# A scan with expert routing: PSUM banks dealt out anew, another order of its loop, other places for loads and weight splits

## The chip, the cores and the metric

The kernel runs on one core of a Trainium2 chip. The metric is the device time of one execution in microseconds (us). All times below are in us unless marked ns. TensorE does the matrix products, VectorE, ScalarE and GpSimd the elementwise work, and SyncE (SP) issues most of the transfers. PSUM, into which TensorE writes, has eight banks.

## The reference

Three stages run one after the other, for 4 batches of 768 positions. The first is a chunked scan with 8 heads (head width 32, state width 16):

```python
log_a = np.log(np.clip(a, 1e-06, 1.0))
for c in range(nc):                                   # chunks of the sequence
    cum = np.cumsum(la, axis=-1)
    L = np.exp(cum[:, :, :, None] - cum[:, :, None, :]) * causal
    y_intra = einsum((Cc @ Bc^T) * L, xc)
    y_inter = einsum(Cc, state) * np.exp(cum)
    state = decay_full * state + sum_j(Bc_j xc_j * decay_from_j)
```

The second is a mixture of 8 experts on the scan's output (256 columns). Each token's expert is the argmax of its 8 logits, or, where a gate lies at 0.5 or above, the expert of the token before it, so the choice is itself a scan over the sequence. The result is `p[e] * (relu(x @ w1[e]) @ w2[e])`. The third adds the real part of a Fourier transform over the sequence and the columns, normalizes, and adds a two-layer product.

## The kernel before

`phase_a` (line 170) holds the scan and the routing; then come the eight experts (line 802), and the third stage (line 1055). Each engine works through its instructions in the order in which the program lists them (`manual_schedule`), and waits only where data or a buffer asks for it.

In `phase_a` the sequence is cut into 6 chunks `c` of 128 positions. One iteration `i` of the loop at line 623 handles a pair: one chunk and two of the four batches (`bp`), so there are 12. Per pair: `prep` makes two masked copies `ch` of `ce` (the C rows times the decay rows), `scores` (line 338) multiplies them with the B rows into four PSUM banks `g0` to `g3`, `mask` (line 352) puts the causal mask on them on VectorE, `carry` (line 361) adds the state's part to `yb`, `intra` (line 373) the masked product with `xt`, `keep` (line 384) copies `yb` out on ScalarE, and `rows` (line 423) turns that copy into rows of tokens with their logits in `tl`, two groups of two products each, which ScalarE copies to `x1n`. `state_mm`, `state_up`, `state_add` and `state_scale` renew the state through `dps`. `xt` (line 332), `ce` (line 277) and `state_add` run on GpSimd.

PSUM: `yb` has two banks. Its first 256 columns per bank take `carry` and `intra`. Its free columns hold `rp` (the routing's transposes), `dps`, `lp` and `rk_ps` (the ranks). Where TensorE writes one bank and another engine reads it, the program makes them wait for each other, whatever the columns are. `tl` has two buffers of one bank.

The decay rows: `decays` works them out from `a` into `e_r`, which is stored to HBM (`e_d`) and loaded again spread over 128 partitions by `load_eb` (line 267), eight transfers of 32 KB for each chunk, in pieces of 512 bytes; chunk 0 is spread by a product instead (`spread0`). The buffers for it in the pool `ald` are two. `load(c)` (line 187) loads the inputs of a chunk into one of three sets of buffers.

Routing: `routing` (line 439) is a generator for one chunk (for the last chunk, half of one). Its steps on VectorE are handed out by `gap`, some between the four masks of an iteration; its steps on TensorE by `place`: the transposes of `kd` (line 469), those of `er` (line 490), and the ranks: a product with `tri` (line 506), one with the counts so far (line 507), and three products (line 513) over the tiles of the chunk. Each product in 32-bit floats stands as two instructions in the trace. At the end each chunk has four scatters (line 556, two with each `leave`) of its token rows to `xs_buf`, sorted by expert; the experts load from there (`xn`, line 732), and that load waits for all 24 scatters.

`load_w` (line 130) loads an expert's two weights into the two buffers `raw`; its generator then splits each into a high part (ScalarE, line 149) and a low part (VectorE and GpSimd, line 151), in four steps. For expert 0 the steps stand at the ends of the iterations 6 to 9. `zfill` (line 300) fills with zeros the rows of `xs_buf` that may stay unused.

## Time and profile before

| | us |
|---|---|
| median of 3 runs (lowest to highest) | 514.0 (511.27 to 516.89) |
| the profiled execution's own time | 515.08 |
| its span, first to last instruction | 513.3 |
| TensorE busy in the span | 466.0 (91%) |
| VectorE busy | 260.0 (51%) |
| ScalarE busy | 191.0 (37%) |
| GpSimd busy | 210.5 (41%) |
| mean granted TensorE clock, as a share of 2.4 GHz | 0.939 |

A busy share is an average over stages with different limits. A row of the timeline names the start, the duration, the engine, the line, the operation, the tile written and the tiles read, and in brackets how long the engine had been idle before and who released it. Durations of merged rows span all their instructions. The products' ends are modelled.

### The profile page before, as it was taken

How to read it: one execution, taken by the hardware profiler on the slowest of the kernel's cores; microseconds unless marked ns; L12 is line 12 of the kernel's file. 1: busy time of each engine (PE TensorE's matmuls, PEld its weight loads, DVE VectorE, ACT ScalarE, POOL GpSimd, SP SyncE). 2: the span in 40 equal slices, each digit the busy share in tenths (PEclk: the TensorE clock that was granted, in tenths of full speed). 3: DMA queues.
4: the chain of work that ended last, by engine and by line, in shares of the span. 5: the costliest groups of instructions: out<-in, count | busy, mean ns of one | idle time of the engine just before them, and what ended most of it. 6: DMA issues, size and time to landing. Idle time of an engine off the chain costs nothing. (4 is left out here: it accounts for less than half of the span.)

```text
span 513.3 us, 9012 instructions
## 1 busy us (share of the span) xinstructions
PE 466.0 (91%) x3481; PEld 396.5 (77%) x3481; DVE 260.0 (51%) x652; ACT 191.0 (37%) x393; POOL 210.5 (41%) x233
## 2 busy tenths in 40 slices
PE   8786787776699999999999999779999999999996
PEld 4564556464389989898989989466898989898986
DVE  3553495533164635455364633098655657574341
ACT  2253253211155454545455443124433243443130
POOL 2233377517138474655738463275430333220000
PEclk9797998565899999999999999989999999999999
DMA  7595823302314553544354410360022201000001
GB/s 242 180 244 162 289 104 125 121 15 91 112 41 130 162 195 131 177 144 144 137 165 134 162 61 18 97 215 23 1 70 104 92 2 43 1 26 17 32 10 43
DMA packets 36899, 54.73 MB, mean 107 GB/s; under 512 B 4013, under 2 KB 27725, under 8 KB 36848
## 3 DMA queue, kind: packets, MB, share of 16 engines
q1 hardware_dynamic: 33296, 46.40, 28.7%
q0 software_dynamic: 3072, 7.46, 4.3%
q8 instruction: 29, 0.48, 0.4%
q10 hardware_dynamic: 480, 0.22, 0.2%
q14 instruction: 22, 0.18, 0.1%
HBM read 42.24 MB, written 12.87 MB: 107 GB/s over the span
## 5 line engine op out<-in xcount | busy, mean ns | idle before, releaser
L703 DVE SCALAR_TENSOR_TENSOR hl<-mm,hh 128x512 fp32r<-128x512 f32 x112 | 77.1, 690 | 77.0 <-ACT hh L702 76.9
L702 ACT ACTIVATE hh<-mm 128x512 fp32r<-128x512 f32 x112 | 66.5, 596 | 90.7 <-PE mm L701 90.7
L710 PE MATMUL mm<-w2h,hh 128*128 128x256 f32 x256 | 72.1, 282 | 0.0
L710 PE MATMUL mm<-w2l,hh 128*128 128x256 f32 x256 | 71.5, 279 | 0.0
L710 PE MATMUL mm<-w2h,hl 128*128 128x256 f32 x256 | 71.5, 279 | 0.0
L750 POOL DMA_INDIRECT y_tok<-y,ids x32 | 34.4, 1076 | 53.1 <-ACT y L749 33.0
L710 PE MATMUL mm<-c2h,hh 128*128 128x256 f32 x192 | 54.4, 284 | 0.0
L710 PE MATMUL mm<-c2h,hl 128*128 128x256 f32 x192 | 53.8, 280 | 0.0
L710 PE MATMUL mm<-c2l,hh 128*128 128x256 f32 x192 | 53.8, 280 | 0.0
L701 PE MATMUL mm<-xh,w1h 128*128 128x512 f32 x128 | 50.9, 398 | 0.0
L701 PE MATMUL mm<-xh,w1l 128*128 128x512 f32 x128 | 50.8, 397 | 0.0
L710 PEld LDWEIGHTS mm<-w2h,hl 128*128 128x128 f32 x256 | 48.5, 189 | 0.0
L710 PEld LDWEIGHTS mm<-w2l,hh 128*128 128x128 f32 x256 | 48.2, 188 | 0.0
L710 PEld LDWEIGHTS mm<-w2h,hh 128*128 128x128 f32 x256 | 48.2, 188 | 0.0
L151 POOL TENSOR_TENSOR w1l<-r,w1h 128x640 fp32r<-128x640 f32 x16 | 30.5, 1905 | 37.8 <-ACT w1h L149 37.8
L701 PE MATMUL mm<-xl,w1h 128*128 128x512 f32 x128 | 40.1, 395 | 0.0
L701 PE MATMUL mm<-xh,c1h 128*128 128x512 f32 x96 | 39.4, 411 | 0.6 <-ACT xh L724 0.6
L701 PE MATMUL mm<-xh,c1l 128*128 128x512 f32 x96 | 38.0, 396 | 0.0
L710 PEld LDWEIGHTS mm<-c2l,hh 128*128 128x128 f32 x192 | 36.2, 188 | 0.1
L710 PEld LDWEIGHTS mm<-c2h,hh 128*128 128x128 f32 x192 | 36.1, 188 | 0.1
L710 PEld LDWEIGHTS mm<-c2h,hl 128*128 128x128 f32 x192 | 36.2, 188 | 0.0
L355 DVE TENSOR_TENSOR mt<-g,ca 128x512 f32<-128x512 f32 x48 | 31.1, 681 | 8.7 <-PE g L346 8.6
(306 smaller groups left out, 904.0 us busy)
## 6 DMA issues: line engine op xcount, KB each, us to landing
r<-in_w_dram SPq DMA_DIRECT2D x16, 1024.0 KB
xn<-xs_buf SPq DMA_DIRECT2D x8, 530.0 KB
rawc<-in_wc_dram SPq DMA_DIRECT2D x8, 512.0 KB
out_dram<-o SPq DMA_DIRECT2D x24, 128.0 KB
z<-y_tok SPq DMA_DIRECT2D x3, 768.0 KB
xs_buf<-scr SPq DMA_DIRECT2D x8, 265.0 KB
c1h<-in_x_dram SPq DMA_DIRECT2D x4, 512.0 KB
xk<-y_tok SPq DMA_DIRECT2D x4, 512.0 KB
```

What stands on the lines that cost most here:

```text
L151: eng.tensor_tensor(out=l_[:, x:y], in0=r_[:, x:y], in1=h[:, x:y], op=ALU.subtract)
L355: V.tensor_tensor(out=m[:, :, 2 * q:2 * q + 2, :], in0=gp[q], in1=cc("cmask").unsqueeze(1).unsqueeze(1).to_broadcast([128, 2, 2, 128]), op ...
L701: PE.matmul(out=ps, lhsT=w[:, d, f * 128:(f + 1) * 128], rhs=x[:, d, :], start=(k == 0), stop=(k == 5))
L702: A.activation(out=hh[:, f, :], in_=ps, func=ACTF.Relu)
L703: V.scalar_tensor_tensor(out=hl[:, f, :], in0=ps, scalar=0.0, in1=hh[:, f, :], op0=ALU.max, op1=ALU.subtract)
L710: PE.matmul(out=ps, lhsT=h[:, f, t * 128:(t + 1) * 128], rhs=w[:, f, :], start=(k == 0), stop=(k == 23))
L750: w = G.indirect_dma_start(out=y_tok, out_offset=bass.IndirectOffsetOnAxis(ap=ids[:, t:t + 1], axis=0), in_=y, in_offset=None, bounds_chec ...
```

## The change

- `rp`, `dps`, `lp`, `rk_ps` and the counts move from `yb` to a bank of their own, `mb`; `tl` has one buffer instead of two.
- `decays`, `columns` and the spreading of chunks 0 and 1 (`spread01`) come in halves, interleaved with the first scores; chunk 1's decay rows no longer go through HBM.
- `e_d` is laid out so that `load_eb` reads pieces of 2 KB; all its 32 transfers stand ahead of the loop, with four buffers. The zero fills move from before the loop into its first four iterations.
- In the loop `mask`, `state_up`, `rows` (now one group per call) and `carry` change places; `place` stands twice between the two groups of `rows`; `gap` gives steps first to chunks that had no `place` in this iteration. The additional `place` calls of the last two iterations go.
- Ranks: one scan over expert and tile (`ac`) replaces three products and the steps `at` and `an`.
- Weights: expert 0's two loads at the iterations 5 and 7, its first two splits at 8 and 9, the other two behind the last scatters; expert 1's loads at 10 and 11. `fa`, `fb`, `rix` at 9 instead of 7.

The diff, cut to its core:

```diff
-            ld = st.enter_context(tc.tile_pool(name="ald", bufs=2))
+            ld = st.enter_context(tc.tile_pool(name="ald", bufs=4))
...
-            rp, dps = yb[:, 0, 256:512], yb[:, 1, 256:384].rearrange("p (u d) -> p u d", u=2)
+            mb = pg.tile([128, 512], FP32, name="mb")
+            rp, dps = mb[:, 0:256], mb[:, 256:384].rearrange("p (u d) -> p u d", u=2)
...
-            warm(4)
+            warm(2)
...
+            def spread01(c, part):
+                ps0 = yb[:, c, :].rearrange("p (b i) -> p b i", b=NB)
+                r = 32 * c
+                if part == 0:
+                    ces[c] = wk.tile([128, NB, 128], FP32, tag="ce", name="ce")
+                for b in range(2 * part, 2 * part + 2):
+                    PE.matmul(
+                        out=ps0[:, b, :], lhsT=bsel[r:r + 32, b, :], rhs=e_r[r:r + 32, 0, 0:128], start=True, stop=True
                     )
+                h = slice(2 * part, 2 * part + 2)
+                V.tensor_tensor(out=ces[c][:, h], in0=ps0[:, h], in1=lds[c]["ct"][:, h], op=ALU.mult)
...
                     SP.dma_start(
-                        out=ebs[c][16 * h:16 * h + 16],
-                        in_=e_d[c * NB:(c + 1) * NB, h, :].unsqueeze(0).to_broadcast([16, NB, 128]),
+                        out=ebs[c][16 * h:16 * h + 16].rearrange("n b i -> n (b i)"),
+                        in_=e_d[c, h].rearrange("b i -> (b i)").unsqueeze(0).to_broadcast([16, NB * 128]),
                     )
...
-                    tl = pg.tile([128, RW], FP32, tag="t", name="tl", bufs=2)
+                tl = pg.tile([128, RW], FP32, tag="t", name="tl")
...
-                oh = sm.tile([128, nb, NE], FP32, tag="oh", name="oh")
+                ot = sm.tile([128, NE, nb + 1], FP32, tag=f"ot{nb}", name="ot")
+                oh = ot[:, :, 1:].rearrange("p e b -> p b e")
                 V.tensor_tensor(out=oh, in0=tb, in1=f_.to_broadcast([128, nb, NE]), op=ALU.is_equal)
+                yield "v", lambda: route["a"] == (c, b0)
+                V.tensor_copy(out=ot[:, :, 0], in_=route["acc"])
                 yield
-                ac = route["acc"]
+                ac = sm.tile([128, NE, nb + 1], FP32, tag=f"ac{nb}", name="ac")
+                V.tensor_tensor_scan(
+                    out=ac.rearrange("p e b -> p (e b)"), data0=again[nb].rearrange("p e b -> p (e b)"),
+                    data1=ot.rearrange("p e b -> p (e b)"), initial=0.0, op0=ALU.mult, op1=ALU.add,
+                )
...
+                PE.matmul(out=rk_ps, lhsT=cc("tri"), rhs=oh, start=True, stop=False)
                 PE.matmul(
-                    out=rk_ps, lhsT=cc("ones"), rhs=ac.unsqueeze(1).to_broadcast([128, nb, NE]),
-                    start=False, stop=False, skip_group_check=True,
-                )
-                for b in range(nb - 1):
-                    n = nb - 1 - b
-                    PE.matmul(
-                        out=rk_ps[:, b + 1:nb, :], lhsT=cc("ones"), rhs=oh[:, b:b + 1, :].to_broadcast([128, n, NE]),
-                        start=False, stop=(n == 1), skip_group_check=True,
-                    )
+                    out=rk_ps, lhsT=cc("ones"), rhs=ac[:, :, 0:nb].rearrange("p e b -> p b e"), start=False, stop=True
+                )
...
-                        if r[1] is None:
+                    for r in sorted(rq, key=lambda r: r[3] == now[0]):
+                        if r[1][0] == "v" and r[1][1]():
...
+            decays(0, 0)
+            spread01(0, 0)
+            spread01(0, 1)
             prep(0)
+            decays(0, 1)
+            columns(0)
             prep_x(0)
+            scores(0)
             prep(1)
             prep_x(1)
-            scores(0)
-            load(1)
-            load_eb(1)
+            decays(1, 0)
+            for q in range(6):
+                SP.dma_start(
+                    out=e_d[q].rearrange("h b i -> b h i"), in_=e_r[32 * (q % 3):32 * (q % 3) + 32, q // 3, 0:128]
+                )
             load(2)
-            load_eb(2)
-            zfill(0)
-            zfill(4)
-            mask(0)
+            for q in range(2, 6):
+                load_eb(q)
+            state_mm(0)
+            for q in range(4):
+                mask(0, q)
+            state_up(0)
+            spread01(1, 0)
+            spread01(1, 1)
+            decays(1, 1)
             kappa0()
             kappa()
+            columns(1)
...
                     load(c + 2)
-                    load_eb(c + 2)
-                if i in (4, 10):
-                    ws = load_w(i // 10)
-                if i == 7:
+                if i < 4:
+                    zfill(2 * i)
+                    zfill(2 * i + 1)
+                if i in (5, 7):
+                    ws = load_w(0, i // 7)
+                if i in (10, 11):
+                    ws1 = load_w(1, i - 10)
+                if i == 9:
...
                 intra(i)
                 keep(i)
-                if more and pairs[i + 1][0] + 1 < NC:
+                if more:
+                    mask(i + 1, 0)
+                    gap(1)
+                    mask(i + 1, 1)
+                    mask(i + 1, 2)
+                if upd:
                     state_mm(i + 1)
+                    state_up(i + 1)
+                if more:
+                    mask(i + 1, 3)
+                rows(i, 0)
                 place()
-                rows(i)
                 place()
+                rows(i, 1)
+                if more:
+                    carry(i + 1)
                 state_add(i)
                 state_scale(i)
...
                 leave()
-                gap(6)
-                if i + 2 >= NP:
-                    place()
-                    gap(4)
-                    place()
-                    if more:
-                        carry(i + 1)
+                gap(7)
...
+                gap(3)
+                if bp == 1 and c + 2 < NC:
+                    spread(c + 2)
+                if i in (8, 9):
+                    next(ws)
...
             while scq:
                 leave(0)
+            for _ in ws:
+                pass
```

## Rows read from the trace of the kernel before

**Rows 1.** Windows by stage: busy of each engine, clock, DMA share, GB/s

```profile
16.30:38.64 22.34, 19.20 (x345) 14.64 (x339) 11.82 (x28) 10.79 (x29) 7.51 (x8) 0.85 0.90 228
38.64:107.69 69.05, 52.31 (x640) 38.54 (x636) 37.79 (x107) 23.63 (x63) 34.05 (x43) 0.79 0.47 149
107.69:130.42 22.73, 15.91 (x86) 10.71 (x83) 6.33 (x49) 2.85 (x12) 13.73 (x21) 0.59 0.19 67
```

**Rows 2.** Windows of three single iterations, the same columns (PE, PEld, DVE, ACT, POOL)

```profile
28.46:33.52 5.06, 4.25 (x93) 3.26 (x89) 3.15 (x10) 2.65 (x8) 1.46 (x2) 1.00 1.12 181
38.64:49.66 11.02, 6.72 (x93) 5.04 (x89) 3.71 (x10) 3.27 (x11) 3.06 (x5) 0.77 0.60 171
92.06:107.69 15.63, 12.20 (x89) 8.62 (x85) 9.06 (x34) 2.40 (x7) 6.67 (x9) 0.50 0.33 103
```

**Rows 3.** Timeline of an undisturbed iteration, TensorE's products and ScalarE's two copies

```profile
28.46 1.15 PE L346 MATMUL g<-ch,c2h 32*128 32x256 f32 x16
...
29.54 1.08 PE L379 MATMUL yb<-mt,xt 128*32 128x128 f32 x32
...
30.69 0.60 ACT L386 ACTIVATE x1t<-yb 128x512 f32<-128x512 f32 x1 [1.05 <-PE yb L379]
...
31.43 0.43 PE L394 MATMUL yb<-xt,c2l 128*32 128x64 f32 x16 [0.81 <-ACT x1t L386]
...
31.79 1.20 PE L433 MATMUL tl<-ca,x1t 128*128 128x137 f32 x8
...
32.56 0.86 ACT L437 ACTIVATE scr<-tl 128x265 f32<-128x265 f32 x2 [1.28 <-PE tl L433]
...
32.92 0.67 PE L368 MATMUL yb<-ce,st 32*64 32x128 f32 x16
```

**Rows 4.** Timeline of two stalls: the decay rows, and carry behind the routing

```profile
42.88 1.26 POOL L277 TENSOR_TENSOR ce<-eb,c1l 128x512 f32<-128x512 f32 x1 [7.32 <-DMA eb<-e_d]
...
44.17 0.91 ACT L324 ACTIVATE ch<-ce,ca 128x256 f32<-128x256 f32 x2 [5.16 <-POOL ce L277]
...
56.84 0.67 PE L368 MATMUL yb<-ce,st 32*64 32x128 f32 x16 [0.51 <-ACT kr L479]
```

**Rows 5.** Waits of VectorE, 16 to 111: total, times, longest

```profile
DVE ro L521 <- PE yb L368: 12.2, 2, 7.4
```

**Rows 6.** Timeline of SyncE's queue: start, time over which issued, count

```profile
9.94 5.47 SPq L270 DMA_DIRECT2D eb<-e_d  x8
...
23.83 5.06 SPq L303 DMA_DIRECT2D xs_buf<-scr  x8
...
33.14 7.96 SPq L270 DMA_DIRECT2D eb<-e_d  x8
...
96.48 0.38 SPq L136 DMA_DIRECT2D r<-in_w_dram  x1
132.13 0.92 SPq L732 DMA_DIRECT2D xn<-xs_buf  x2
```

**Rows 7.** All transfers into `eb`: duration of one issue, ns, least, median, most

```profile
L270 SPq DMA_DIRECT2D eb<-e_d x38: 302/414/1038, 9.9 to 59.0; - x38
```

**Rows 8.** Timeline of the prologue, VectorE's second reciprocal

```profile
5.97 0.95 DVE L247 RECIPROCAL e_r<-f_r 96x128 f32<-96x128 f32 x1 [0.44 <-ACT e_r L232]
```

**Rows 9.** Groups by line and form, 16.3 to 107.69: busy, mean ns, idle before

```profile
L355 DVE TENSOR_TENSOR mt<-g,ca 128x512 f32<-128x512 f32 x44 | 28.6, 681 | 6.4 <-PE g L346 6.3
L513 PE MATMUL yb<-oh,cb 128*128 128x24 f32 x8 | 2.0, 328 | 0.0
```

**Rows 10.** Groups of GpSimd by line, 16.3 to 131, the same columns

```profile
L556 POOL DMA_INDIRECT xs_buf<-scr,si x24 | 24.1, 1006 | 7.8 <-issue 5.2 <-POOL scr L554 2.6
L151 POOL TENSOR_TENSOR w2l<-r,w2h 128x640 fp32r<-128x640 f32 x2 | 3.1, 1544 | 4.9 <-ACT w2h L149 4.8
```

**Rows 11.** Timeline of the tail: the last scatter, and the first work on `xn`

```profile
129.42 0.97 POOL L556 DMA_INDIRECT xs_buf<-scr,si  x1 [0.30 <-issue]
...
136.30 0.16 DVE L739 SCALAR_TENSOR_TENSOR ids<-xn,out_of 128x4 int32<-128x4 int32 x1 [10.62 <-DMA xn<-xs_buf]
```

More of the change, by code (lines that the diff above doesn't have):

```diff
@@ L228, in phase_a, with decays @@
             f_sb = big.tile([128, 24, NH], FP32, name="f_sb")
-            e_d = dram.tile([24, NH, 128], FP32, name="e_d")
+            e_d = dram.tile([NC, NH, NB, 128], FP32, name="e_d")
             lt = big.tile([96, 2, 64], FP32, name="lt")
             V.memset(zz, 0.0)
-            A.activation(out=e_r[:, 0, 0:1], in_=zz[:, 0:1], func=ACTF.Exp)
+            tw = big.tile([96, 1], FP32, name="tw")
+            A.activation(out=tw, in_=zz[:, 0:1], func=ACTF.Exp)
             V.memset(f_r[:, :, 63:64], 1.0)
-            def decays():
-                V.tensor_scalar(out=ar, in0=ar, scalar1=1e-6, scalar2=1.0, op0=ALU.max, op1=ALU.min)
-                for q in range(2):
+            def decays(q, part):
+                if part == 0:
+                    V.tensor_scalar(out=ar[:, q], in0=ar[:, q], scalar1=1e-6, scalar2=1.0, op0=ALU.max, op1=ALU.min)
                     V.tensor_tensor_scan(
@@ L243, in decays @@
                     )
-                V.tensor_copy(out=f_r[:, :, 0:63], in_=lt[:, :, 1:64])
-                V.tensor_copy(out=e_r[:, :, 128:129], in_=lt[:, :, 0:1])
-                V.reciprocal(out=f_r[:, :, 64:128], in_=e_r[:, :, 64:128])
-                V.reciprocal(out=e_r[:, :, 0:64], in_=f_r[:, :, 0:64])
-            def columns():
-                for q in range(2):
-                    ps0 = pg.tile([128, 512], FP32, tag="t", name="ps0", bufs=2)
-                    PE.transpose(ps0[:, 0:96], f_r[:, q, :], ident[0:96, 0:96])
-                    A.activation(
-                        out=f_sb[:, 12 * q:12 * q + 12, :].rearrange("p u h -> p (u h)"), in_=ps0[:, 0:96], func=ACTF.Copy
-                    )
@@ L257, in phase_a @@
-            ces, ebs = {}, {}
-            def spread0():
-                ps0 = pg.tile([128, NB, 128], FP32, tag="t", name="eb", bufs=2)
-                for b in range(NB):
-                    PE.matmul(out=ps0[:, b, :], lhsT=bsel[:, b, :], rhs=e_r[0:32, 0, 0:128], start=True, stop=True)
-                ces[0] = wk.tile([128, NB, 128], FP32, tag="ce", name="ce")
-                V.tensor_tensor(out=ces[0], in0=ps0, in1=lds[0]["ct"], op=ALU.mult)
+                    V.tensor_copy(out=f_r[:, q, 0:63], in_=lt[:, q, 1:64])
@@ new lines, in decays, with columns @@
+                    V.reciprocal(out=e_r[:, q, 0:64], in_=f_r[:, q, 0:64])
+                else:
+                    V.reciprocal(out=f_r[:, q, 64:128], in_=e_r[:, q, 64:128])
+                    V.tensor_copy(out=e_r[:, q, 128:129], in_=lt[:, q, 0:1])
+            def columns(q):
+                ps0 = pg.tile([128, 512], FP32, tag="t", name="ps0")
+                PE.transpose(ps0[:, 0:96], f_r[:, q, :], ident[0:96, 0:96])
+                A.activation(
+                    out=f_sb[:, 12 * q:12 * q + 12, :].rearrange("p u h -> p (u h)"), in_=ps0[:, 0:96], func=ACTF.Copy
+                )
@@ L530, in routing @@
                 )
-                yield
-                at = sm.tile([128, NE], FP32, tag="at", name="at")
-                V.tensor_reduce(out=at, in_=oh.rearrange("p b e -> p e b"), axis=AX.X, op=ALU.add)
-                yield
-                an = sm.tile([128, NE], FP32, tag="ac", name="ac")
-                V.tensor_tensor(out=an, in0=ac, in1=at, op=ALU.add)
-                route["acc"] = an
-                route["a"] = (c, 2) if nb < NB and not b0 else (c + 1, 0)
                 yield
@@ L569, in step @@
                 try:
[L570 removed]
+                    r[1] = next(r[0]) or ("v", lambda: True)
                 except StopIteration:
@@ L585, in place @@
                 for r in sorted(rq, key=lambda q: q[2]):
-                    if r[1] is not None and r[1]():
+                    if r[1][0] == "p" and r[1][1]():
+                        r[3] = now[0]
                         step(r)
@@ L634, in phase_a @@
                     SP.dma_start(out=rix, in_=io["rix"])
+                upd = more and pairs[i + 1][0] + 1 < NC
                 if more:
@@ L659, in phase_a @@
                 leave()
-                gap(6)
-                if i + 2 >= NP:
-                    place()
-                    gap(4)
-                    place()
-                    if more:
-                        carry(i + 1)
-                if bp == 1 and c + 2 < NC:
-                    spread(c + 2)
+                gap(7)
                 if c + 1 == NC:
```

122 lines of the change are left out of this document (58 added, 64 removed).

## The prediction

> **What bounds the kernel now.** I read the windows by stage first. The first expert's matmuls start at 137.86; what comes before is the scan with the routing, and only there does the diff touch anything. In [rows 1] look at TensorE's busy time beside the length of each stretch, and at the granted clock behind it. The two expert stages after 137.86 are left alone, so every gain or loss is a shift of that start. The chain of waits as answered reaches back only to the late expert stages, so the scan is read from windows and timelines.
>
> The loop has twelve iterations (pairs of batches). Eleven of them, from the scores of the second pair at 16.30 to the last `intra` at 107.69, take 22.34 for the first four and 69.05 for the next seven, 9.86 each [rows 1]. In those seven no engine is full: over seven iterations TensorE 52.31 (7.5 each, at a mean clock of 0.79, so about 5.9 at the full 2.4 GHz), VectorE 37.79 (5.4), GpSimd 34.05 (4.9), ScalarE 23.63 (3.4). So waits bound it, and a clock that falls in them. [rows 2] shows both ends: an undisturbed iteration takes 5.06 at clock 1.00, one with the inputs late 11.02 at 0.77, the last but one 15.63 at 0.50 (1.2 GHz).
>
> The undisturbed one [rows 3] is a chain on TensorE: scores, intra, a hole of 0.74 (31.43 less 30.69) while ScalarE copies `yb` out, then state products, the two `tl` rows, carry. State products wait for that copy although they read nothing of it: `dps` lies in the same bank.
>
> Two stalls recur. The decay rows arrive late: `ce` waited for `eb`, ScalarE's `ch` for `ce`, and the copy of `yb` stands behind `ch` on ScalarE [rows 4]. And the routing shares `yb` with the state: carry waits for ScalarE's reading of `kr` [rows 4], VectorE's `ro` for carry, up to 7.4 at once and 12.2 in two waits [rows 5], and all masks stand behind `ro` on VectorE; scores and intra wait for masks. The SP queue shows the first stall's root: eight zero fills issued from 23.83, then the inputs of chunk 3, and its `eb` loads only from 33.14 to 41.10 [rows 6].
>
> **The change, part by part.** *Prologue.* `e_r` of the first half no longer waits for both full reciprocals (0.95 for the second, behind a wait of 0.44 for ScalarE's table load, [rows 8]); half a reciprocal remains before `spread01`. That frees the 0.44, the 0.95 of the first (of the same size), half of the second and some of the scans, 2.3. Against it, chunk 1's `ce` in two halves and the last half reciprocal now stand before the first scores of the loop, about 1.1 with their hand-offs. I take 1.2 earlier; ends 2.3 earlier and 1 later.
>
> *First four iterations.* No stall to remove in most; they pay the single `tl` bank. `tl` had two buffers, now one: the second row group waits for ScalarE's copy of the first. From [rows 3]: half of 1.20 is 0.60, so the first would end at 32.39; ScalarE starts at 32.56 (0.17 later), needs 0.43, and some 0.14 pass until TensorE resumes (x1t ends at 31.29, L394 starts at 31.43): 0.74. Queued behind it are the second `tl`, carry and the next scores. Against it the state products (0.36 until `tl` starts) move into the hole, since `dps` is in `mb` now. Net 0.4 per iteration: 1.6 lost.
>
> *The seven.* 5.06 + 0.4 = 5.46. Routing on TensorE fills the new hole first, since both `place` calls stand between the two row groups. Of the rank products the L513 group goes, six instructions per chunk, of which the two of one form cost 2 x 328 ns [rows 9], 2.0 per chunk as recorded and mostly at the low clock; about 0.8 at the full one. What is left, some 1.4 per chunk or 0.7 per iteration, lies in a hole of 0.74, but unevenly; I add 0.25: 5.7. VectorE does four masks of 681 ns [rows 9] first and routing after them; its load of 5.4 falls a little, because two of the four splits of expert 0's weights move behind the loop; the new copy and scan take the place of `at` and `ac`. Where the scan of `er` waits for `kr` it lags by some 0.4: 6.1. GpSimd: 34.05 less two splits (3.1), plus 3.7 of issue time about its twelve scatters, is 34.7, 5.0 each [rows 1, 10]. But a chunk's four scatters (1.0 and 0.3 of issue each, [rows 10]) fall into one iteration, and the last `ce` stands behind them on GpSimd, `ch` and the copy of `yb` behind `ce` on ScalarE: I take 2 once, between nothing and 5.2. Sum 7 x 6.1 + 2 = 44.7 against 69.05, a gain of 24.3. The bounds: 5.06 each (35.4), and 8 each (56) if half of today's waiting returns.
>
> *Decay rows.* Chunk 1's come by matmul. The other four chunks' `eb` loads go out at once, before the zero fills, since `ald` has four buffers. Eight of them took 5.47 to issue with inputs ahead and 7.96 behind the zero fills [rows 6]; one alone takes 414 ns in the median [rows 7]. After the first eight (done about 16, since the inputs of chunk 2 stand before them) 24 more cost 10 to 16, four zero fills 2.5, so chunk 3's inputs go out between 29 and 35; they are needed at some 38. I count the stall as gone; if the slow issue holds, up to 4 comes back. The Trainium skill (DMA: Bandwidth & Descriptors, Measured) speaks against this part: transfers under 64 KB are dominated by their descriptors, and an `eb` transfer stays at 32 KB whatever its pieces. By that rule the rows would be no sooner, and the sum would be 504 instead of 500. No row shows 2 KB pieces of this transfer.
>
> *Tail.* Twelve scatters remain when the loop ends, before and after: the last ends at 130.39 [rows 11], 22.7 behind 107.69. The extra `place` calls of the last two iterations are gone, so chunks 4 and 5 have two to three routing steps more to do behind the loop. A copy out of PSUM with its two hand-offs is 0.74 [rows 3], with VectorE's part about 1 per step: 3 later; ends 0 and 5.
>
> *Weights.* Half of expert 0's splits now run on GpSimd behind the last scatter: 2 x 1.54 [rows 10] plus hand-offs, 3.4. The second weight half of expert 1 reuses the buffer they read, so its transfer waits for them, and on the SP queue the load of `xn`, which the first expert needs, stands behind that transfer. Before, it had gone out at 96.48, and `xn` at 132.13, 1.74 after the last scatter [rows 6, 11]. Now `xn` goes out some 4.1 after it: 2.4 lost. Then 1 MB is ahead of it in the queue. Both `xn` loads, 1.06 MB, were in by 136.30, at most 4.2 after their issue [rows 6, 11]; the megabyte costs between 2 and 4.2; I take 3.6. Together 6 (ends 2.4 and 6.6).
>
> **Sum**: -1.2 + 1.6 - 24.3 + 3 + 6 = -14.9. Against the profiled execution's 515.08 (its span 513.3 and 1.8 around it) that is 500; it lies 1.1 above the median of 514.0, so 499 to 500 there. I say 500.
>
> **The rivals.** *The clock stays down (slower).* TensorE's prologue has holes, and of six warming products two are left. If the loop runs at 1.2 GHz throughout, the 4.25 of TensorE's work in an undisturbed iteration [rows 2] becomes 8.5, plus 0.74 and some handing over, about 10: 7 x 10 = 70 is 1 more than now, and 10.6 is lost elsewhere, less 1.2: 525. It decides from a mean iteration of 8.5 on. For it: 15.63 at 0.50 [rows 2], where waits kept the clock down. Against it: with one hole of 0.74 in every iteration the clock was 1.00 [rows 2, 3]; two such holes are what no row shows. The Trainium skill (TensorE: Matmul & The Clock Gate, A second HAM failure mode) describes just this, a kernel whose short idles between groups of matmuls, from cycling through PSUM banks, made the clock swing between its two levels; the trace so far disagrees for one hole. Chance 0.12.
>
> *Another wait takes the place.* GpSimd's lumps, late inputs or a `ro` that still stands before masks: 8 per iteration. 13 gained, 10.6 lost, 1.2 gained: 511. For it: GpSimd's 5.0 is close to the pace already, and [rows 5] shows how long one blocked instruction holds VectorE. Chance 0.16.
>
> *The pace is better and the weights cost nothing.* 5.2 per iteration (36.4), the tail as before, `xn` 2 later: 485. For it: 5.06 was reached with all loads running. Chance 0.12. The change not doing what it says, the decay rows coming no sooner, is the case of 504, inside the forecast's own range.
>
> **How the numbers follow.** The forecast has 0.60, its own range 493 to 507 (iterations of 5.3 to 6.9 alone make 494 to 506, and the ends of tail and weights add a little). The range for 8 in 10 takes in most of the better case and the part of the next rival below 513: 487 to 513. A measurement of this kernel can tell about 1%, 5 us. Faster by more: 0.60 + 0.12 and a bit of the wait rival, 0.74; within 1%: 0.14; slower: 0.12.
>
> **What would show it.** Right: between the second scores and the last `intra` seven iterations of 5.5 to 6.5 at a clock near 1.00; no wait of `ro` for carry, none of carry for `kr`; `ce` without a wait for `eb`; two `tl` copies apart; `xn` issued 4 or more after the last scatter, behind the weight transfer. Wrong: a clock of 0.5 in the loop, GpSimd full with scatters before the last iteration, or `tl` waits above 1. The forecast fails if the mean iteration is over 8.5, or if the first `xn` is in more than 15 behind the last scatter.

## The result and the profile after

The changed kernel takes 499.5 us in the median of four runs (497.57 to 500.04), the kernel before 514.0 (511.27 to 516.89). The ratio is 0.971 with a 95% interval of 0.965 to 0.977: faster by 2.9%. The profiled execution took 499.32 with a span of 497.5. Two of the four runs of one variant below (`ch` behind the copy) were in the chip's slow state, so its time is that of the other two.

The first expert's products now start at 122.49 instead of 137.86. From there to the end 375.01 are left, 375.4 before. So the whole gain lies in the stage that the diff touches, 15.4. The windows of the changed kernel, cut at the same points as [rows 1]: the prologue, the first four iterations, the next seven, from the last `intra` to the end of the last scatter, and from there to the first expert. The columns are the busy time and number of instructions of PE, PEld, DVE, ACT and POOL, then the granted clock, the DMA share and GB/s.

```profile
0.00:16.66 16.66, 10.98 (x56) 6.27 (x57) 8.79 (x33) 3.51 (x8) 3.62 (x8) 0.77 0.74 244
16.66:39.93 23.27, 19.67 (x339) 14.85 (x339) 13.23 (x30) 10.95 (x31) 5.24 (x6) 0.87 0.52 135
39.93:86.14 46.21, 36.51 (x611) 27.61 (x607) 33.98 (x93) 21.48 (x59) 25.82 (x34) 0.89 0.63 192
86.14:110.40 24.26, 14.99 (x85) 8.96 (x81) 8.93 (x60) 5.34 (x16) 18.42 (x28) 0.72 0.34 126
110.40:122.49 12.09, 1.83 (x9) 1.57 (x9) 0.50 (x4) 0.60 (x1) 3.03 (x3) 0.53 0.60 188
```

Look at the third line beside the second of [rows 1]: 46.21 instead of 69.05, with TensorE's busy time down from 52.31 to 36.51 mostly because the clock rose from 0.79 to 0.89; that the rank products are fewer is a small part (37.83 with the old ones put back, below). Term by term, measured against the sum:

| Term | predicted | measured | from |
|---|---|---|---|
| prologue (first scores of the loop) | -1.2 | +0.4 | 16.66 less 16.30 |
| first four iterations | +1.6 | +0.9 | 23.27 less 22.34 |
| next seven | -24.3 | -22.8 | 46.21 less 69.05 |
| tail, to the end of the last scatter | +3 | +1.6 | 24.26 less 22.70 |
| weights and `xn` | +6 | +4.3 | 10.2 less 5.9 from last scatter to first work on `xn` |

The measured terms add up to -15.7 before rounding; 0.3 are lost again between the first work on `xn` and the first product, which leaves the 15.4.

An undisturbed iteration, 59.15 to 64.56, takes 5.41 at clock 1.00 and has the routing of a chunk in it. Those of its TensorE and ScalarE rows that stand around the copy of `yb` and the row products, to be read against [rows 3]:

```profile
61.12 0.41 PE L412 MATMUL mb<-xt,c2l 128*32 128x64 f32 x16
...
61.43 0.60 ACT L404 ACTIVATE x1t<-yb 128x512 f32<-128x512 f32 x1 [1.11 <-PE yb L397]
...
62.08 0.73 PE L450 MATMUL tl<-ca,x1t 128*128 128x137 f32 x4 [0.55 <-ACT x1t L404]
62.65 0.31 PE L532 MATMUL mb<-ot,cb 128*128 128x32 f32 x2
62.79 0.40 PE L533 MATMUL mb<-ac,cb 128*128 128x32 f32 x2
62.85 0.39 ACT L454 ACTIVATE scr<-tl 128x265 f32<-128x265 f32 x1 [0.82 <-PE tl L450]
63.02 0.39 PE L486 MATMUL mb<-ca,kd 128*4 128x128 f32 x2
63.30 0.73 PE L450 MATMUL tl<-ca,x1t 128*128 128x137 f32 x4
```

The state products (L412) now run ahead of the copy of `yb`. The second `tl` starts 1.22 after the first: with one buffer it cannot come sooner, since ScalarE's copy ends at 63.24. Three groups of routing products stand in that hole and cost nothing. Where there is no routing the hole is plain, a wait of 0.5.

Six iterations of the loop have that pace. The others are 4 and 5 (7.12 and 6.69), 8 and 9 (9.08 and 7.04), and the very first (7.10, at a clock of 0.59). Two stalls stand behind iterations 4 and 5, 8 and 9. First iteration 4, which starts at 39.93, and the SP queue that leads to it:

```profile
14.80 18.25 SPq L285 DMA_DIRECT2D eb<-e_d  x32
33.15 2.00 SPq L317 DMA_DIRECT2D xs_buf<-scr  x4
35.20 0.71 SPq L197 DMA_DIRECT2D c1l<-in_ct_dram  x1
...
41.53 1.27 POOL L292 TENSOR_TENSOR ce<-eb,c1l 128x512 f32<-128x512 f32 x1 [7.62 <-DMA c2h<-in_bt_dram]
42.83 0.91 ACT L344 ACTIVATE ch<-ce,ca 128x256 f32<-128x256 f32 x2 [2.53 <-POOL ce L292]
43.65 0.57 ACT L404 ACTIVATE x1t<-yb 128x512 f32<-128x512 f32 x1
44.27 0.73 PE L450 MATMUL tl<-ca,x1t 128*128 128x137 f32 x4 [1.96 <-ACT x1t L404]
```

All 32 transfers of decay rows are issued at 0.57 each ahead of chunk 3's inputs, which go out from 35.20. `ce` had waited for `eb` before [rows 4]; now it waits for the inputs and starts 1.35 earlier than then, 41.53 instead of 42.88. The chain behind it is the old one: `ce`, `ch`, the copy of `yb`, the row products.

Then iteration 8, which starts at 64.56:

```profile
65.16 0.98 POOL L567 DMA_INDIRECT xs_buf<-scr,si  x1 [0.30 <-issue]
66.16 1.29 POOL L292 TENSOR_TENSOR ce<-eb,c2h 128x512 f32<-128x512 f32 x1
67.37 0.20 POOL L511 COPY scr<-cb 128x4 int32<-128x4 int32 x1
67.52 0.46 POOL L429 TENSOR_TENSOR sn<-st,sn 128x128 f32<-128x128 f32 x1
67.93 1.04 POOL L352 TENSOR_TENSOR xt<-c1l,f_sb 128x512 f32<-128x512 f32 x1
...
65.46 3.57 DVE L470 TENSOR_TENSOR ls<-scr,mx 128x32 f32<-128x32 f32 x1
68.95 0.68 DVE L374 TENSOR_TENSOR mt<-g,ca 128x512 f32<-128x512 f32 x1
```

`ce` stands behind four scatters on GpSimd, as the prediction had it. But there is a second thing that it had not: VectorE's small `ls`, 0.19 in other places, takes 3.57 and ends at 69.03, together with GpSimd's last instruction (68.97) of an unbroken run. The masks of the next pair stand behind it.

At the end of the stage:

```profile
110.42 3.03 POOL L157 TENSOR_TENSOR w2l<-r,w2h 128x640 fp32r<-128x640 f32 x2
113.48 0.38 SPq L140 DMA_DIRECT2D r<-in_w_dram  x1
113.96 1.07 SPq L754 DMA_DIRECT2D xn<-xs_buf  x2
120.60 0.16 DVE L761 SCALAR_TENSOR_TENSOR ids<-xn,out_of 128x4 int32<-128x4 int32 x1 [8.12 <-DMA xn<-xs_buf]
```

The splits run behind the last scatter, the weight transfer waits for them, and `xn` goes out behind it, 3.56 after the last scatter (before 1.74, [rows 11] and [rows 6]).

### The profile page after: what moved, and what is told of

Same layout as the page of the kernel before. It is cut to its first block, busy times and chain, and to the rows that moved or that the text cites. A ratio compares the mean times of both kernels' runs of the same rounds, so it can differ in the third digit from the quotient of the medians.

```text
span 497.5 us, 8957 instructions
## 1 busy us (share of the span) xinstructions
PE 448.2 (90%) x3447; PEld 383.9 (77%) x3447; DVE 264.1 (53%) x664; ACT 191.4 (38%) x393; POOL 208.7 (42%) x232
## 4 chain that ended last, share of the span: by engine, by line
PE 69%; POOL 9%; DMA 8%; issue 7%; SPq 4%; DVE 2%; ACT 1%; POOLq 0%; ACTq 0%
PE mm L723 32%; PE mm L732 29%; POOL xs_buf L567 3%; PE tp L744 3%; SPq L285 2%; DMA xk<-y_tok 2%; PE f L954 2%; DMA xn<-xs_buf 1%; DMA c2l<-in_bn_dram 1%; DMA c2h<-in_bt_dram 1%; DMA y_tok<-y,ids 1%; DMA bsel<-in_bsel_dram 1%; PE g L366 1%; PE cps L968 1%; POOL w1l L157 1%
```

## Which part of the change made the gain

Each run is given with its median and its ratio to the kernel before on its own chip; the chips differ a little, so the windows of the stage carry the comparisons. "The seven" is the stretch from iteration 4's scores to the last `intra`: 69.05 before, 46.21 after.

**The banks taken back.** `mb` becomes a view of the second bank of `yb`, `rp` goes back into the first, `tl` has two buffers:

```diff
-            mb = pg.tile([128, 512], FP32, name="mb")
-            rp, dps = mb[:, 0:256], mb[:, 256:384]...
+            mb = yb[:, 1, :]
+            rp, dps = yb[:, 0, 256:512], mb[:, 256:384]...
-                tl = pg.tile([128, RW], FP32, tag="t", name="tl")
+                tl = pg.tile([128, RW], FP32, tag="t", name="tl", bufs=2)
```

> The changed kernel with its PSUM banks dealt out as before: rp, dps, the ranks and the totals lie in the two banks of yb again, tl has two buffers again; order of work, decay rows, rank scan and weights as changed. Theory (the banks carry the gain): carry waits again for the routing's reading of kr, ro for carry, and the masks stand behind ro; the seven iterations go from 46.2 back to 62 to 69, the first four win 0.4 each from the second tl buffer: 513 to 521 us. Rival (the new order of place, carry and masks carries it): the pace holds, seven iterations of 45 to 49, 498 to 503 us.

Measured: 501.45, ratio 0.976 (0.972 to 0.980). Its windows, first four and seven, and what `ro` waits for carry (total, times, longest):

```profile
19.29:41.01 21.72, 18.53 (x340) 13.90 (x339) 13.72 (x31) 11.00 (x32) 5.21 (x6) 1.00 0.48 113
41.01:86.97 45.96, 35.36 (x610) 26.67 (x606) 33.91 (x90) 21.29 (x59) 25.91 (x34) 0.93 0.60 193
...
DVE ro L541 <- PE yb L386: 0.6, 2, 0.3
```

The seven take 45.96. The theory that the new banks carry the gain falls: with the old banks and the new order nothing is lost in the loop, and `ro` waits 0.6 for carry where it waited 12.2 [rows 5]. The first four are 1.55 shorter. Of these 0.7 belong to the three iterations behind the first (5.06, 5.05 and 5.35 against 5.35, 5.41 and 5.41), near the 0.4 each that the prediction worked out for the second `tl` buffer; the other 0.8 belong to the first one (6.26 against 7.10), which the runs with the single buffer and this order have anywhere between 6.32 and 7.10. What the old banks cost is in the prologue: first scores at 19.29, where the run with `xn` first, whose spreads of chunk 0 are as slow (1.19 and 1.22), has them at 18.14. The first expert starts at 122.88, 0.4 later than in the changed kernel; the rest of the difference in span, 1.6, lies behind that, where the two are alike.

**The banks alone**, in the kernel before: `mb` as a bank of its own, `tl` single; `rp`, `dps`, ranks and totals moved there.

> The kernel before with the banks of the change alone: a bank mb of its own for rp, dps, ranks and totals, one tl buffer. Theory (the banks carry the gain): no wait of ro for carry and none of carry for kr; the seven iterations fall from 69 to 46 to 52, the first four lose 0.4 each; with weights and tail as before 493 to 500 us, that is at least as fast as the whole change. Rival (the order carries it): 508 to 516 us.

Measured: 503.25, ratio 0.977 (0.972 to 0.983). The seven, and what VectorE waited for in them (total, times, longest):

```profile
39.31:96.31 57.00, 47.23 (x640) 34.81 (x636) 33.85 (x100) 23.36 (x63) 32.65 (x41) 0.85 0.50 165
...
DVE ro L522 <- ACT kr L480: 11.4, 3, 4.5
```

The time lies between the two expectations. Half of the gain: no `ro` waits for carry any more, but `ro` still stands ahead of masks and waits, now for ScalarE's `kr`, 11.4 in all (12.2 for carry in [rows 5]).

**The masks first, alone**, in the kernel before:

```diff
-                    gap((0, 1, 2, 2)[q])
...
                     if pairs[i + 1][0] + 1 < NC:
                         state_up(i + 1)
+                    gap(5)
```

> The kernel before with one turn of VectorE's order: the four masks and the state's product sn of an iteration stand ahead of the routing's steps, as in the changed kernel; banks, carry, place, decay rows and weights as before. Theory (the stall is masks standing behind a waiting ro; with the new order alone the banks as before gave the same pace): ro may wait as long as before, but TensorE no longer waits for masks, the seven iterations fall from 69 to 46 to 55: 497 to 503 us. Rival (the shared bank makes carry and ro wait for each other whatever stands behind them, and only the new places of the routing's products between the rows cure it): seven iterations of 60 to 69, 506 to 514 us.

Measured: 507.15, ratio 0.987 (0.982 to 0.991), the rival's time.

```profile
37.00:96.81 59.81, 44.37 (x641) 33.62 (x637) 36.36 (x107) 23.97 (x63) 33.72 (x43) 0.83 0.54 180
...
DVE sn L401 <- PE yb L367: 13.9, 3, 8.8
```

With the masks ahead of the routing the wait goes on in another place: `sn` reads the bank that carry writes, carry stands ahead of it in TensorE's order, and VectorE waits 13.9 for it. In the changed kernel `state_up` comes before carry in the program. That is why the banks taken back did no harm there: carry comes after `sn`, and after both row groups, when the routing's bank has long been read. So two waits had been stacked, masks behind `ro` and `sn` (or `ro`) behind carry. The new order takes away both; the new banks alone, or the masks alone, one each. What the places of the routing's products between the two row groups are worth by themselves was not run, nor was the new order alone in the kernel before: that it carries the gain follows from taking out, one at a time, the banks, the early rows and the rank scan, none of which gives back much of the seven (45.96, 43.92 and 46.61 against 46.21).

**Decay rows and zero fills as before**, in the changed kernel: two `eb` buffers, chunk 2's rows and all zero fills ahead of the loop, `load_eb(c + 2)` beside `load(c + 2)`.

> The changed kernel with the decay rows and zero fills in the places that they had before: two buffers, rows of chunk 2 and all eight zero fills ahead of the loop, the rows of a later chunk behind its inputs inside the loop; pieces of 2 KB, banks and order of work as changed. Theory (the early rows are a part of the gain of their own: with the order of the masks alone, or the banks alone, iteration 4 still took 12.2 and 9.4): ce waits for eb again, iteration 4 or 5 takes 9 to 12 instead of 7, the seven iterations 50 to 57, 503 to 510 us. Rival (the order leaves enough slack that the rows may come as before): seven iterations of 45 to 48, 498 to 501 us.

Measured: 498.5, ratio 0.967 (0.960 to 0.974). The rival was right.

```profile
40.43:84.35 43.92, 35.07 (x610) 26.71 (x606) 32.49 (x94) 21.36 (x59) 25.69 (x34) 0.92 0.50 168
...
41.22 1.28 POOL L292 TENSOR_TENSOR ce<-eb,c1l 128x512 f32<-128x512 f32 x1 [6.81 <-DMA eb<-e_d]
```

`ce` waits for `eb` again, starts at 41.22 (41.53 with the rows early), and iteration 4 takes 6.02 against 7.12. The early rows are worth nothing: what they gain the inputs lose on the same queue.

**Pieces of 512 bytes**, in the changed kernel: `e_d` laid out as before, the same 32 transfers.

> The changed kernel with the decay rows stored and read in pieces of 512 bytes as before; the same 32 transfers in the same places. Theory (the queue issues by the count of transfers, 0.57 us each, whatever the pieces): the issues still end at about 33, chunk 3's inputs go out at about 35, the same time within 1 us. Rival (the pieces set the pace, 0.7 to 1.0 us each as in the kernel before): chunk 3's inputs 4 to 14 us later, iteration 4 longer by as much, 503 to 512 us.

Measured: 498.1, ratio 0.970 (0.966 to 0.974): the same time, as the theory had it, and the queue's row too (18.25 with 2 KB pieces):

```profile
13.75 18.83 SPq L285 DMA_DIRECT2D eb<-e_d  x32
```

**The old rank sums**, in the changed kernel: L513's products, `at` and `an` instead of the copy and the scan.

> The changed kernel with the tile counts as before: three more rank products per chunk (L513's form), at and an on VectorE instead of the copy and the scan. Theory, from the sum: 0.8 us of TensorE per chunk at full clock that no longer fits into the hole behind tl, and the totals handed on later in the tail: 1 to 4 us slower than the changed kernel, 500 to 504 us. Rival: TensorE has room for it in its waits, and the same time within 1 us.

Measured: 505.89, ratio 0.982 (0.976 to 0.988), above both expectations. The seven and the tail:

```profile
40.11:86.72 46.61, 37.83 (x640) 29.01 (x636) 34.12 (x89) 21.53 (x59) 26.09 (x34) 0.93 0.60 183
86.72:114.38 27.66, 18.16 (x85) 11.70 (x85) 9.52 (x65) 5.32 (x16) 18.41 (x28) 0.69 0.30 110
```

In the loop 0.4, in the tail 3.4: 27.66 against 24.26. There the totals of chunk 4 are handed on only after `at` and `an`, and GpSimd sits from the fourth scatter (issued to 93.0) to the fifth at 98.16, where the changed kernel has its fifth at 93.86. The first expert starts at 126.45, 4.0 later. The spans lie further apart, 504.3 against 497.5: the other 2.8 are found behind that point, in stages that are alike.

## What still stands in the way, and a faster version

**`xn` first.** The second weight half of expert 1 is sent for after the two `xn` loads:

```diff
-                if i in (10, 11):
-                    ws1 = load_w(1, i - 10)
+                if i == 10:
+                    ws1 = load_w(1, 0)
...
                     xn = load_x(pools, e + 1)
+                if e == 0:
+                    load_w(1, 1)
```

> The changed kernel with the second weight half of expert 1 sent for only after the two xn loads have gone out; nothing else moved. Theory (the splits' buffer and the megabyte ahead of xn cost the 4.3 us between 10.2 and 5.9 from the last scatter to the first work on xn): xn goes out some 1.7 after the last scatter and is there 5.9 to 6.5 after it, 494 to 496 us. Rival (the megabyte only moves: it then competes with xn, or its splits come too late for the second expert): 497 to 500 us.

Measured: 494.9, ratio 0.967 (0.961 to 0.973). `xn` goes out 1.69 after the last scatter (its end at 110.72) and is worked on 5.6 after it, against 10.2:

```profile
112.41 0.93 SPq L754 DMA_DIRECT2D xn<-xs_buf  x2
113.79 0.37 SPq L140 DMA_DIRECT2D r<-in_w_dram  x1
...
116.32 0.16 DVE L761 SCALAR_TENSOR_TENSOR ids<-xn,out_of 128x4 int32<-128x4 int32 x1 [3.59 <-DMA xn<-xs_buf]
```

From the first product to the end it is 375.0 as in the changed kernel, so the late megabyte holds up nobody.

**Inputs first on the queue.** Chunk c+3's inputs in the second iteration of chunk c, the rows of chunks 4 and 5 behind them in iterations 1 and 3, zero fills in 2 to 5:

```diff
-                if bp == 0 and c and c + 2 < NC:
-                    load(c + 2)
+                if bp == 1 and c + 3 < NC:
+                    load(c + 3)
+                if i in (1, 3):
+                    load_eb(4 + i // 2)
```

> The changed kernel with the queue's order alone turned: chunk c+3's inputs go out in the second iteration of chunk c, the decay rows of chunks 4 and 5 behind them in iterations 1 and 3, zero fills in iterations 2 to 5. Theory (iteration 4 stalls because 32 issues of 0.57 stand ahead of chunk 3's inputs): ce of chunk 3 without a wait of 7, iteration 4 falls from 7.1 to 5.4 and 5 from 6.7 to 5.4 with the clock at 1.00: 496 to 497 us. Rival (late inputs are hidden, iteration 4 is long for another reason): within 0.5 us of the changed kernel.

Measured: 497.5, ratio 0.973 (0.965 to 0.982). Iterations 4 and 5 take 5.41 each, and the seven are 3.2 shorter:

```profile
41.45:84.47 43.02, 34.77 (x610) 26.59 (x606) 32.28 (x92) 21.37 (x59) 22.90 (x30) 0.92 0.55 168
```

`ce` of chunk 3 starts at 36.22 there and waits for no transfer. How much of the 3.2 this is worth is less sure, since the loop also started 1.5 later in this profile (first scores at 18.18), and a late loop meets late inputs with less harm: the run with `xn` first, with the queue as in the changed kernel and first scores at 18.14, has its `ce` as late as 41.56 and still takes 5.43 and 5.41 for iterations 4 and 5, and pays in 6 and 7 (6.11 and 6.89). Over iterations 4 to 7 the inputs first are 2.2 shorter than that run, 3.0 shorter than the changed kernel; the three edits together, below, reach iteration 4 at 39.91, as the changed kernel does, and have the four at 5.41. The late start takes half of the gain back, and the ratio shows none of it (0.973 against 0.971).

**ScalarE's `ch` put behind the copy of `yb`**, the row copies and the state scaling:

```diff
-                if i + 2 < NP:
-                    prep(i + 2)
                 intra(i)
...
                 state_scale(i)
+                if i + 2 < NP:
+                    prep(i + 2)
```

> The changed kernel with ScalarE's ch (prep) put behind the copy of yb, the row copies and the state scaling, so that a late ce holds up no copy of yb. Theory A (a late ce makes both long iterations, by ScalarE's order alone): 4 and 8 fall to 5.4 to 5.7, no wait of tl for x1t over 1, 493 to 495 us. Theory B (iteration 8 is long because VectorE's ls is held for 3.6 while GpSimd runs from instruction to instruction): 4 falls, 8 stays at 7.5 to 9, ls again takes 2 to 4, 496 to 498 us.

Measured: 507.95 and 510.57; the kernel before beside it has a median of 511.59, so next to nothing of the gain is left. Both theories missed what the move does:

```profile
47.50 1.15 PE L366 MATMUL g<-ch,c2h 32*128 32x256 f32 x16 [1.15 <-ACT ch L344]
...
67.39:74.02 6.63, 4.92 (x94) 3.86 (x94) 4.61 (x6) 3.14 (x9) 5.84 (x8) 1.00 0.25 86
```

The scores need `ch` at the head of the next iteration. At the end of ScalarE's order it is late each time, mostly by 1.15, and ten iterations pay. Iteration 4 has no stall now (6.63 like its neighbours), but the slower loop also comes to it later (47.50 instead of 39.93), when `ce` of chunk 3 is done (41.49). Iteration 8 takes 7.80, and VectorE's `er` lasted 3.62 there: the lateness on ScalarE is not all of iteration 8.

**`ce` of chunk 5 on VectorE:**

```diff
-                G.tensor_tensor(out=ces[c], in0=ebs[c], ...
+                (V if c == 5 else G).tensor_tensor(out=ces[c], in0=ebs[c], ...
```

> The changed kernel with one product moved: ce of chunk 5, 1.29 us on GpSimd behind the four scatters of iteration 7, is made by VectorE. Theory A (ScalarE's ch waits for that ce): no wait of ch, no wait of tl for x1t in iteration 8. Theory B (VectorE held by GpSimd's unbroken run): the run is shorter by 1.3 and ls is held for 1 to 2.3 instead of 3.6. Both: iteration 8 falls from 9.1 to 5.5 to 7, 495 to 497 us. Rival (VectorE has no room for it, or the run lasts as long with the scatters alone): iteration 8 stays above 8.5, 498 to 500 us.

Measured: 496.92, ratio 0.973 (0.967 to 0.979); iteration 8 takes 6.82 instead of 9.08.

```profile
39.64:83.21 43.57, 35.36 (x610) 26.65 (x607) 31.21 (x90) 21.38 (x59) 24.89 (x33) 0.92 0.63 205
...
65.94 0.83 DVE L292 TENSOR_TENSOR ce<-eb,c2h 128x512 f32<-128x512 f32 x1 [0.18 <-issue]
66.25 0.57 POOL L511 COPY scr<-cb 128x4 int32<-128x4 int32 x1
```

Now it is VectorE that got in first, and GpSimd's copy, 0.20 elsewhere, takes 0.57 and ends with VectorE's `ce`. The run does not part the two theories, since the edit serves both. The ratio of the whole time, 0.973 against 0.971, does not show the 2.6 that the seven are shorter.

**Three warming products more**, in holes of TensorE in the prologue:

> The changed kernel with three warming products more, each in a hole of TensorE in the prologue: one behind chunk 0's spread, one between the halves of chunk 1's, one behind it. Theory (the prologue and the first iteration of the loop run at 1.2 GHz because four warming products and the products of kappa were given up): the loop's first scores come at 15.0 to 16.5, the first iteration falls from 7.1 to 5.4 to 6, 495 to 497 us. Rival (the products only stand in the way): first scores at 17 to 19, first iteration as before or 1 shorter, 498 to 501 us.

```diff
             spread01(0, 1)
+            warm(1)
...
             spread01(1, 0)
+            warm(1, <a tile of tag "t">)
             spread01(1, 1)
+            warm(1, <a tile of tag "t">)
```

Measured: 497.86, ratio 0.974 (0.968 to 0.980), the rival's case: first scores at 18.36, first iteration 6.55. The products of chunk 0's scores and of chunk 1's spreads were as slow as in the changed kernel or slower (2.09, and 1.22 each), so the clock did not rise, and the first scores came later than in the six other profiles whose first spreads were as fast (16.48 to 17.63): the products stood in the way. By accident the run shows more of iteration 8: the same run of GpSimd instructions, `ce` as late as ever, but VectorE had come to its masks by then and not to `ls`. GpSimd runs without a break from 64.13 to 67.94; the masks are not slowed, and `cand`, 0.17 in most other places, ends with it at 68.01:

```profile
41.08:82.82 41.74, 33.80 (x611) 25.75 (x607) 30.72 (x90) 21.36 (x59) 25.91 (x34) 0.96 0.64 205
...
65.37 1.28 DVE L374 TENSOR_TENSOR mt<-g,ca 128x512 f32<-128x512 f32 x2
...
67.36 0.65 DVE L476 SCALAR_TENSOR_TENSOR cand<-ls,cb 128x32 f32<-128x32 f32 x1
```

Iteration 8 took 7.10. So of its 3.7 beyond the pace in the changed kernel about 2 belong to the held `ls`, some 1.7 to the late `ce`; one run each, not a controlled pair.

**The three edits together** (`xn` first, inputs first, chunk 5's `ce` on VectorE):

> The changed kernel with three edits together: the second weight half of expert 1 behind xn, the inputs ahead of decay rows and zero fills, chunk 5's ce on VectorE. Theory (the three costs are apart: the wait for xn 4.2, iterations 4 and 5 3.2, iteration 8 2.3): seven iterations of 40 to 41.5, the first work on xn 5.6 to 6.3 behind the last scatter, 487 to 490 us. Rival (they overlap: what the loop gains is lost in the tail, or GpSimd, now at its pace, makes a new wait): 491 to 494 us.

Measured: 491.65 (488.37 to 494.19), ratio 0.960 (0.954 to 0.966), the fastest of all kernels here.

```profile
39.91:79.52 39.61, 32.45 (x611) 24.97 (x607) 30.81 (x91) 21.25 (x59) 20.60 (x28) 1.00 0.63 188
```

The seven at 5.7 each at clock 1.00 (iteration 8 is 7.10, the others 5.41 to 5.70), work on `xn` 5.6 behind the last scatter, the first product at 111.87, 10.6 earlier than in the changed kernel. In this profile the costs are apart and nearly add up: 6.6 in the seven, 4.6 for `xn`, of which 0.5 are lost in the tail. By the whole time it is less clear: the four runs are 488.4, 489.6, 493.7 and 494.2, so the profiled one is in the theory's range and the median in the rival's, 1.7 above the theory's. What differs between its runs is open, since only one has a trace.

## Why the prediction was right, and where its steps were not

The total came out as forecast, 499.5 against 500, and the term that carries it, the seven, by 1.5. The four small terms were each off by 0.7 to 1.7, one too hopeful and three too dark, and with the seven they nearly cancel: that the total came within 0.5 is luck in good part, while the size of the main term is not. Of the signs that the prediction had set for itself, `ro` and carry waited for each other no more and the clock rose, but only to 0.89; the mean of the seven, 6.60, lies just over its 5.5 to 6.5, `xn` went out 3.56 after the last scatter and not 4, and waits of `tl` above 1, a sign of being wrong, came in iterations 4 and 8 (1.96 and 1.98). By its steps:

- *An undisturbed iteration of 5.46.* 5.41 was measured. The step from [rows 3], that the second `tl` waits for ScalarE's copy and the state products move into the hole, held; the 0.7 of routing per iteration fits into the hole with nothing added, and the lag of 0.4 on VectorE did not show. The reserve of 0.25 and 0.4 per iteration (4.6 over seven), with the 2 for GpSimd's lump, went instead to two stalls that cost 8.3. So the seven came out with the wrong reserve and nearly the right amount.
- *The cause of the stall.* The prediction read the waits of [rows 4, 5] as those of a shared bank and of masks behind `ro`, and priced both cures as one. The runs part them: the changed kernel with the banks as they were has hardly any of either wait (0.6 of `ro` for carry), the banks or the masks alone cure one of the two. That the shared bank had to be left was wrong; it was enough to ask it in another order.
- *"I count the stall as gone" (decay rows).* Wrong. The condition that the prediction gave itself, slow issues, held: 0.57 each. Chunk 3's inputs went out at 35.2, just past its 29 to 35, and iterations 4 and 5 cost 3.0 over the pace, inside its "up to 4". The 2 KB pieces changed nothing, 18.83 against 18.25 for the same 32 transfers. The Trainium skill (DMA: Bandwidth & Descriptors, Measured) says that transfers under 64 KB are dominated by their descriptors. That pieces of 2 KB would therefore not help is the prediction's own reading of it, and the two runs bear that reading out; the 504 that it worked out from there did not come, since rows as late as before cost nothing in the new order.
- *GpSimd's lump, 2 once.* Place and chain were right (`ce` behind the scatters, `ch` waits 2.55, the rows 1.98), the size was not: 3.7 in iteration 8 and 1.6 more in 9 at a clock of 0.75. The term lacked VectorE being held, though the trace of the kernel before had that too: `kd` took 4.81 there (the rows are in the last section).
- *Tail, +3.* It measured +1.6, and the step's premise failed: not twelve scatters remain when the loop ends but sixteen of the 24, and GpSimd is busy 18.42 in the tail against 13.73 [rows 1]. The last twelve take 16.5, much as before (17.0); what grew is the time ahead of them, from 5.7 to 7.7, in which the four others run. Without the rank scan the tail would have been +5.0 (27.66 less 22.70, also with sixteen scatters), and the scan gives back 3.4, since the totals reach the next chunk sooner. The prediction had the scan's gain in the loop, where it is 0.4.
- *Weights, +6.* It measured 4.3: the issue 1.8 later (2.4 taken) and the megabyte 2.5 (3.6 taken, bounds 2 to 4.2). For the megabyte, the upper half of the range was the mistake; the order of the queue was right, and `xn` first took it all back.
- *Prologue, -1.2.* Wrong in sign. Nine profiles with this prologue have the first scores between 16.48 and 18.18, the three with the old one between 15.36 and 16.30. The chain on VectorE got shorter as worked out, but TensorE ran at 0.50 from 10 to 20, where before it had 1.00 up to 15; the step missed that each spread of chunk 1 then takes 1.22 instead of 0.7 and VectorE's `ce` waits for it. In three of the nine the first spread already took 1.19 instead of 0.68, and these have the latest first scores, 17.95 to 18.18. The rows are from the changed kernel:

```profile
13.47 1.22 PE L276 MATMUL yb<-e_r,bsel 32*128 32x128 f32 x4 [1.33 <-DVE ce L280]
14.72 0.42 DVE L280 TENSOR_TENSOR ce<-yb,c1l 128x256 f32<-128x256 f32 x1 [1.31 <-PE yb L276]
```

Of the rivals, the low clock kept to single iterations (6.6 in the mean, far from 8.5), and two holes of about 0.5 in each of the three iterations from 23.76 to 39.93 left it at 1.00; "another wait takes the place" happened in small: iterations 4, 5, 8 and 9 cost 8.3 over the pace of 5.41, where the rival had all seven at 8; the better pace without the cost of the weights is what the three edits came near to, with 39.6 in the seven where the rival had 36.4.

## What to carry to other kernels

Where two producers share a bank, look first at the order in which the engines' programs ask for it: with the masks ahead of the routing and carry behind `sn` and the row products, the old banks did no harm here, while a bank of its own in the old order cured only half. On a queue that issues in order, count the issues ahead of the transfer that is needed next, not the bytes: rows for chunks 4 and 5 sent early made chunk 3's inputs late, and a weight that nobody needed yet stood ahead of `xn`. Before an instruction is moved to an engine's end because it may be late, ask when its product is wanted: `ch` moved behind the copies cost about 1.15 in ten iterations.

## What the runs showed of the hardware

**VectorE and GpSimd hold each other.** In the changed kernel and in seven of its variants one small VectorE instruction in iteration 8 took 3.40 to 3.87. It was issued 0.2 to 0.5 into the scatter that begins GpSimd's unbroken run and ended with the run's last instruction (`er`, itself 0.47 long, 0.3 later). The kernel before has the same, and the run with the masks first (`er`, 3.04). Before, GpSimd runs from 66.72 to 72.10:

```profile
67.32 4.81 DVE L464 SCALAR_TENSOR_TENSOR kd<-kd,ff 128x4 f32<-128x4 f32 x1
...
70.84 1.26 POOL L277 TENSOR_TENSOR ce<-eb,c2h 128x512 f32<-128x512 f32 x1
```

Which instruction it hit changed with the run: `ls` (two operands in SBUF), `si`, `sx` (one operand), `er`. Masks, whose first operand lies in PSUM, ran beside the same GpSimd instructions at 0.64 each, as fast as ever, and so did the reduction `px` (0.17 at 65.28, in the run with three warming products). Where VectorE was first, GpSimd's copy waited instead (0.57 for 0.20). The Trainium skill (SBUF — State Buffer, SBUF: two separate sides) has it that the two engines share a pair of ports as an exclusive lock, taken by whichever instruction starts first and held for that whole instruction; on VectorE's side it names instructions with two operands in SBUF and those in a two-port mode. The runs agree on the lock, and on the operands for `ls`, `si`, `er` and the masks; whether `sx` ran in such a mode no trace shows. They differ in its length: `ls` was held through five instructions of GpSimd, not one. What lets the lock pass between two GpSimd instructions at other times (other scatters, with a gap of 0.3 behind them, held nobody, and `ls`, issued 0.28 into the scatter that begins the run, took its 0.19 in the run with three warming products) stays open.

**A busy TensorE at the low clock.** In the run with three warming products more TensorE was busy for all of 10 to 20 and the granted clock was 0.50 in both halves of that stretch (1.2 GHz); in the kernel before it was busy 4.74 of the 5.00 from 5 to 10 and 2.43 of the next 5.00, and had 1.00 (2.4 GHz) through both. The difference lies earlier: both had 1.00 up to 5 and then 0.86 against 1.00, with holes of 0.5 around the first spread in the one and four warming products in a row in the other. Whether two warming products given back at the very start would keep the clock up was not run. One and the same prologue also came out both ways: chunk 0's first spread took 0.68 to 0.71 in six profiles and 1.19 in three (late rows, `xn` first, inputs first). In these three the column of the granted clock reads 1.00 from 5 to 20, although the loop's first scores took 2.09, as they do at 0.50, and not 1.15: there the durations, and not the column, tell the level.
